# Issuing the scatters of output rows one step later, behind GpSimd's next weight split

## The chip, the cores and the metric

One core of a Trainium2 chip. The metric is device time in microseconds (us), median of the runs; lower is better. The engines are named as the profile names them: PE (TensorE, matmuls), DVE (VectorE), ACT (ScalarE), POOL (GpSimd), SP (SyncE, which issues most of the DMAs).

## What is computed

A causal convolution over 7 positions with softmaxed weights per head, then a mixture of 8 experts with a fixed capacity. Each of the 28,672 tokens goes to one expert, chosen greedily by the gate's logits; every expert takes 3,584 tokens and runs a two-layer network on them. Cut to what matters:

```python
x = conv(x, softmax(weight))               # (28672, 192)
logits = x @ w_gate                        # (28672, 8)
assigned = greedy(logits, cap=28672 // 8)  # best logit first, one expert a token
for e in range(8):
    mask = assigned == e
    h = np.maximum(x[mask] @ w1[e], 0.0)   # w1: 192 x 1024
    out[mask] = h @ w2[e]                  # w2: 1024 x 192
```

## The kernel before

**The three parts.** From 0 to about 175 us the kernel convolves 16 blocks of rows into a DRAM buffer `attn` and computes the gate's logits. Then come the experts' networks, to the end. The routing (thresholds, lists of token numbers) is a background job, cut into pieces which a planner (`Pace`, `Steps`) sets in between the matmuls of the other two parts, until some 670 us. The planner counts what PE, DVE and ACT have to do by a table of costs; it doesn't count POOL.

**The tiles.** `FFN.run` (L1294) goes over 56 tiles of 512 tokens of one expert. The order of the tiles is written out by hand: first one tile of each expert (tiles 0 to 7), since only the tokens that are sure of their expert are listed by then, then the others in runs of an expert. Every engine takes its instructions in the order in which the program issues them.

**One tile, eight steps.** In iteration i, step f (0 to 7) issues: layer 1 of tile i for 128 of the 1,024 hidden units (`l1`: five matmuls into `ph`, a ReLU on ACT that writes `hh`, and on DVE the rest `hl`, for products in two parts of reduced precision); a step of the preparation of tile i + 1 (`prep`: gathered rows are transposed and split into `xa`, `xd`); half a block of layer 2 of tile i - 1 (`l2`: eight matmuls into `y`). Background work goes in between. At the end of each step comes one weight split (`wsplit`), if one is due.

**Gathers and scatters.** Both are indirect DMAs, and POOL issues them (they stand in POOL's queue and take about 1 us of it each). `gather` (L1174, its DMAs at L1179) fetches the 512 rows of tile i + 2 at the head of iteration i, four DMAs into one of two buffers `xg`. `store` (L1240) ends a block of 128 tokens of tile i - 1 in steps 1, 3, 5 and 7: ACT copies one half of `y` to `yt`, DVE adds the other and writes `yo` (three buffers), and POOL scatters `yo` to the output's rows (L1247).

**Weight splits.** The weights are loaded as float32 and split into a high and a low part. A piece (128 x 512 or 128 x 384 elements) goes through one of four buffers `raw`: SP issues its load (L1115 to L1120), ACT writes the high part, POOL or DVE subtracts it and writes the low part (L1160), SP copies both to DRAM for a later use by the same expert, and the load of the piece four further on is issued, into the buffer that is free now. An expert has eight pieces. They are split in the first eight iterations alone, one in each step: in steps 0 to 3 the four pieces of layer 2 (POOL's), in 4 to 7 the pieces of the next expert's layer 1 (POOL's in 4 and 6, DVE's in 5 and 7, `dl`). Later the experts' split weights are read back from DRAM without POOL.

So in the first iterations POOL's queue holds four gathers, four scatters and six splits for each tile, and a scatter stands in it at the end of the step's layer 2, ahead of that step's split. A scatter at the head of the queue waits for its `yo`.

Of the kernel before, what the change touches and what calls it, by code (L numbers as in the profile page):

```python
# [28 lines left out]
class Meter:  # L29


    def __init__(self, pace, name, eng):
        self.pace, self.name, self.eng = pace, name, eng
# [40 lines left out]
class Steps:  # L74
# [6 lines left out]
    def run(self, n=1):  # L81

        for _ in range(n):
            while len(self.gens) > self.keep:
                v = next(self.gens[0], self)
                if v is not self:
                    break
                self.gens.pop(0)
            else:
                return  # L90
            p = self.pace
            self.need = p.dve + p.lat if v == PEW else max(p.dve, p.act) + p.lat if v == PEA else v
# [965 lines left out]
class FFN:  # L1058
# [3 lines left out]
    def __init__(self, tc, nc, attn, w1, w2, out, ident, wr, drm):  # L1062
        self.tc, self.nc = tc, nc

        self.kept1 = [drm.tile([128, 3, F], F32, name="kw%d" % e) for e in range(NE)]
        self.keptd = [drm.tile([64, F], F32, name="kd%d" % e) for e in range(NE)]
        self.kept2 = [drm.tile([128, 8, 2 * D], F32, name="kv%d" % e) for e in range(NE)]
        self.attn, self.w1, self.w2, self.out, self.ident, self.wr = attn, w1, w2, out, ident, wr
        self.bg = lambda: None
        self.busy = lambda: False  # L1070
        self.WT, self.RAW, self.XG, self.XT, self.H, self.Y, self.XS = {}, {}, {}, {}, {}, {}, {}
        self.wpa, self.wpb, self.DL = [None, None], [None, None], [None, None]
        self.scat = []
        self.free = set()
        self.xg = None

# [163 lines left out]
    def store(self, i, b, idx):  # L1240
        nc = self.nc
        y = self.Y.pop((i, b))
        t = self.op.tile([128, D], F32, name="yt", bufs=2)
        o = self.op.tile([128, D], F32, name="yo")
        nc.scalar.activation(t, y[:, D:2 * D], AF.Copy)
        nc.vector.tensor_tensor(o, y[:, 0:D], t, op=OP.add)
        st = nc.gpsimd.indirect_dma_start(  # L1247
            out=self.out, out_offset=bass.IndirectOffsetOnAxis(ap=idx, axis=0), in_=o, in_offset=None,
            bounds_check=NTOK - 1, oob_is_err=False)
        for s in self.scat:  # L1250
            self.tc.declare_no_dep(st.ins, s.ins, reason="rows of other tokens")
        self.scat.append(st)
# [41 lines left out]
    def run(self, idx_of, at, eng, free):  # L1294


        tiles = self.tiles
        n = len(tiles)
        for i in range(n + 1):
            at(i)  # L1300
            if i + 2 < n:
                self.gather(i + 2, idx_of(tiles[i + 2], True))
            for f in range(8):
                if i < n:
                    self.l1(i, tiles[i][0], f)
                self.bg()
                if i + 2 < n and f == 6 and free():
                    self.free.add(i + 2)
                if i + 1 < n:
                    self.prep(i + 1, f)  # L1310
                if i:
                    self.l2(i - 1, tiles[i - 1][0], f // 2, f % 2)
                    if f % 2:
                        self.store(i - 1, f // 2, idx_of(tiles[i - 1])[f // 2])
                        if f == 7:
                            self.H.pop(i - 1)
                self.bg()
                if i < n:
                    self.wsplit(i, eng(f))

# [241 lines left out]
```

## Time and profile before

| | |
|---|---|
| Time, median of 3 runs | 1320.28 us (1318.41 to 1320.54) |
| The profiled execution's own time | 1319.91 us |
| Its span in the profile | 1318.1 us |
| PE busy | 1253.2 us, 95% of the span |
| DVE busy | 1001.2 us, 76% |
| ACT busy | 547.7 us, 42% |
| POOL busy | 544.8 us, 41% |
| Granted PE clock, mean | 0.98 |

A row of the profile's timeline gives the start and the length of an instruction, its engine, its line, its operation and `output<-inputs`, and in brackets how long the engine had been idle ahead of it and what ended that. Nearly all rows of PE, DVE and ACT carry L55, the line of the helper that records them; they are told apart by the names of their tiles. The time of a scatter or gather on POOL is that of its issue; the transfer follows. A matmul's time is modelled, and PE's clock is lowered after it has been idle.

### The profile page before, as it was taken

Reading aid. Unit: us, or ns where it says so; the run is one execution under the profiler, and the core shown is the slowest. Engines: PE = TensorE matmul, PEld = TensorE weight load, DVE = VectorE, ACT = ScalarE, POOL = GpSimd, SP = SyncE. Lnnn points to the kernel's source line nnn. Section 1 sums busy time; section 2 is a strip of 40 time slices with the busy share of each in tenths; the row PEclk is TensorE's granted clock in tenths of the full one; section 3 lists DMA queues with packets and bytes.
Section 4 is the critical chain, followed back from the end, with each engine's and each line's share of the span. In section 5 each row is a group of like instructions: output and inputs, shape, how many; then the busy total and the mean of one; then the engine's idle time right before and its main releaser. Section 6 shows DMA issues by size and latency. Waiting matters only on the chain.

```text
span 1318.1 us, 21815 instructions
## 1 busy us (share of the span) xinstructions
PE 1253.2 (95%) x7879; PEld 1076.2 (82%) x7879; DVE 1001.2 (76%) x2215; ACT 547.7 (42%) x1214; POOL 544.8 (41%) x549
## 2 busy tenths in 40 slices
PE   5789979989899999999999999999999999999997
PEld 3345558878788888888889999999999999999997
DVE  6478558769899988998657777777777777777772
ACT  5444543565444443443333333334333343333432
POOL 3000446476643434534224444444444444444422
PEclk9989998999899999999999999999999999999999
DMA  9999977488742432433222441432323222141100
GB/s 241 302 287 300 295 257 253 156 269 271 228 167 93 149 134 94 149 117 116 73 84 93 139 148 48 149 102 87 108 85 101 94 93 90 49 146 49 40 28 30
DMA packets 92932, 188.30 MB, mean 143 GB/s; under 512 B 12353, under 2 KB 57873, under 8 KB 88593
## 3 DMA queue, kind: packets, MB, share of 16 engines
q1 hardware_dynamic: 63888, 120.75, 29.4%
q0 software_dynamic: 21504, 44.07, 11.0%
q10 hardware_dynamic: 7424, 22.02, 4.4%
q8 instruction: 63, 1.03, 0.3%
q14 instruction: 53, 0.43, 0.1%
HBM read 114.44 MB, written 72.35 MB: 142 GB/s over the span
## 4 chain that ended last, share of the span: by engine, by line
PE 79%; DVE 9%; DMA 4%; issue 3%; SPq 2%; POOL 1%; ACT 1%; POOLq 0%; DVEq 0%; ACTq 0%
PE ph L55 35%; PE y L55 35%; PE bg L55 4%; PE cv L55 3%; DVE X L55 3%; DMA X<-in_x_dram 2%; DVE hl L55 2%; DMA raw<-in_moe_w_dram 1%; PE pl L55 1%; PE px L55 1%; DVE aT L55 1%; SPq L187 1%; DMA attn<-a 1%; SPq L167 1%; SPq L190 1%
## 5 line engine op out<-in xcount | busy, mean ns | idle before, releaser
L55 PE MATMUL y<-w,hh 128*128 128x384 f32 x1792 | 546.6, 360 | 0.0
L55 ACT ACTIVATE hh<-ph 128x512 fp32r<-128x512 f32 x448 | 267.4, 597 | 487.6 <-PE ph L55 389.0
L55 PE MATMUL y<-w,hl 128*128 128x192 f32 x1792 | 452.4, 252 | 0.0
L55 DVE SCALAR_TENSOR_TENSOR hl<-ph,hh 128x512 fp32r<-128x512 f32 x448 | 307.7, 688 | 177.4 <-ACT hh L55 145.7
L55 PE MATMUL ph<-xa,w 128*128 128x512 f32 x1344 | 399.4, 405 | 9.4 <-DVE hl L55 9.4
L55 PEld LDWEIGHTS y<-w,hh 128*128 128x128 f32 x1792 | 341.1, 190 | 25.1 <-issue 7.2
L55 PEld LDWEIGHTS y<-w,hl 128*128 128x128 f32 x1792 | 345.6, 193 | 15.4
L1247 POOL DMA_INDIRECT out_dram<-yo,ib x128 | 128.4, 1003 | 293.4 <-DVE yo L55 278.6
L55 PEld LDWEIGHTS ph<-xa,w 128*128 128x128 f32 x1344 | 221.5, 191 | 30.3 <-DVE hl L55 10.7
L1247 POOL DMA_INDIRECT out_dram<-yo,ia x96 | 106.9, 1113 | 247.3 <-DVE yo L55 213.8
L55 DVE STREAM_TRANSPOSE xs<-xg 32x256 f32<-32x256 f32 (+1 forms) x512 | 188.7, 369 | 8.8
L55 PE MATMUL ph<-xd,w 128*128 128x512 f32 x448 | 179.5, 401 | 1.6 <-DVE xd L55 1.1
L55 PE MATMUL ph<-xd,dl 128*128 128x512 f32 x448 | 176.9, 395 | 2.5 <-DVE dl L55 2.2
L1179 POOL DMA_INDIRECT xg<-attn,jb x128 | 130.0, 1016 | 40.1 <-issue 39.8
L55 PE MATMUL cv<-X,TH 118*128 118x384 f32 x256 | 103.1, 528 | 22.2 <-DVE TH L55 12.8
L1179 POOL DMA_INDIRECT xg<-attn,ja x96 | 107.8, 1123 | 28.9 <-issue 25.2
L55 ACT ACTIVATE yt<-y 128x192 f32<-128x192 f32 x224 | 73.2, 327 | 109.0 <-PE y L55 97.8
L55 DVE TENSOR_TENSOR yo<-y,yt 128x192 f32<-128x192 f32 x224 | 79.5, 355 | 47.4 <-ACT yt L55 43.0
L55 PEld LDWEIGHTS ph<-xd,dl 128*128 128x128 f32 x448 | 85.1, 190 | 24.1 <-DVE dl L55 3.8
L55 PEld LDWEIGHTS ph<-xd,w 128*128 128x128 f32 x448 | 84.9, 190 | 22.9 <-DVE xd L55 1.8
L55 PEld LDWEIGHTS cv<-X,TH 118*128 118x128 f32 x256 | 46.0, 200 | 55.0 <-issue 22.6
L55 ACT ACTIVATE a<-cv 128x384 f32<-128x384 f32 x128 | 61.5, 490 | 58.0 <-PE cv L55 51.7
(235 smaller groups left out, 974.0 us busy)
## 6 DMA issues: line engine op xcount, KB each, us to landing
w<-kw SPq DMA_DIRECT2D x16, 1536.0 KB
w<-kv SPq DMA_DIRECT2D x16, 1536.0 KB
X<-in_x_dram SPq DMA_DIRECT2D x16, 1344.0 KB
attn<-a ACTq DMA_DIRECT2D x16, 1344.0 KB
kw<-w SPq DMA_DIRECT2D x48, 256.0 KB
kv<-w SPq DMA_DIRECT2D x32, 384.0 KB
raw<-in_moe_w_dram SPq DMA_DIRECT2D x32, 192.0 KB
raw<-in_moe_w_dram SPq DMA_DIRECT2D x16, 256.0 KB
```

Source lines behind the costliest of these rows:

```text
L55: return f(*a, **k)
L167: nc.sync.dma_start(wgr[32 * pb:32 * pb + 32], wg.rearrange("(c f) e -> f c e", f=32))
L187: nc.sync.dma_start(t[0:6, 1:16], bass.AP(tensor=x.tensor, offset=o + (W - 6) * D, ap=[[D, 6], [W * D, 15], [1, D]]))
L190: nc.sync.dma_start(t[0:6], bass.AP(tensor=x.tensor, offset=o - 6 * D, ap=[[D, 6], [W * D, 16], [1, D]]))
L1179: self.nc.gpsimd.indirect_dma_start(out=t[:, b], out_offset=None, in_=self.attn[0:rows], in_offset=bass.IndirectOffsetOnAxis(ap=idx[b], ax ...
L1247: st = nc.gpsimd.indirect_dma_start(out=self.out, out_offset=bass.IndirectOffsetOnAxis(ap=idx, axis=0), in_=o, in_offset=None, bounds_chec ...
```

## The change

`store` no longer issues the scatter. It puts `yo` and its row numbers into a list, and a new function `scatter` takes them from there and issues the DMA. `run` calls it at the end of the even steps, after that step's weight split. So the scatter of step 1 is issued in step 2, that of step 3 in step 4, that of step 5 in step 6, and that of step 7 in step 0 of the next iteration, behind that iteration's four gathers. In the iteration behind the last tile, the one of step 7 is issued in step 7 itself.

```diff
@@ __init__
-        self.scat = []
+        self.scat, self.late = [], []
@@ store
         nc.vector.tensor_tensor(o, y[:, 0:D], t, op=OP.add)
-        st = nc.gpsimd.indirect_dma_start(
+        self.late.append((o, idx))
+
+    def scatter(self):
+
+        if not self.late:
+            return
+        o, idx = self.late.pop()
+        st = self.nc.gpsimd.indirect_dma_start(
             out=self.out, out_offset=bass.IndirectOffsetOnAxis(ap=idx, axis=0), in_=o, in_offset=None,
             bounds_check=NTOK - 1, oob_is_err=False)
@@ run, at the end of a step
                 if i < n:
                     self.wsplit(i, eng(f))
+                if not f % 2 or i == n and f == 7:
+                    self.scatter()
```

The order of the instructions on PE, DVE, ACT and SP is the same as before; POOL's alone changes. There, in the second iteration that has both scatters and splits, stood before (L1160 is a split, `w2` a piece of layer 2 and `w1` one of layer 1; L1247 is a scatter of the `yo` with that number; `x4` stands for a tile's four gathers):

```order
L1160 TENSOR_TENSOR w2_2392<-raw_2234,w2_2392 128x2x192
L1247 DMA out_0_dram<-yo_2456,ia0_105 28672x192
L1160 TENSOR_TENSOR w2_2392<-raw_2266,w2_2392 128x2x192
L1160 TENSOR_TENSOR w2_2392<-raw_2292,w2_2392 128x2x192
L1247 DMA out_0_dram<-yo_2581,ia0_105 28672x192
L1160 TENSOR_TENSOR w2_2392<-raw_2325,w2_2392 128x2x192
L1160 TENSOR_TENSOR w1_2672<-raw_2396,w1_2672 128x512
L1247 DMA out_0_dram<-yo_2698,ia0_105 28672x192
L1160 TENSOR_TENSOR w1_2672<-raw_2531,w1_2672 128x512
L1247 DMA out_0_dram<-yo_2794,ia0_105 28672x192
L1179 DMA xg_2806<-attn_62,ja0_109 128x192 x4
L1160 TENSOR_TENSOR w2_2839<-raw_2677,w2_2839 128x2x192
```

and there stands now, at the same place of POOL's queue (the scatters have L1254; the numbers of `yo` are the same in both, those of the other tiles are a few lower):

```order
L1160 TENSOR_TENSOR w2_2389<-raw_2231,w2_2389 128x2x192
L1254 DMA out_0_dram<-yo_2315,ia0_105 28672x192
L1160 TENSOR_TENSOR w2_2389<-raw_2263,w2_2389 128x2x192
L1160 TENSOR_TENSOR w2_2389<-raw_2289,w2_2389 128x2x192
L1254 DMA out_0_dram<-yo_2456,ia0_105 28672x192
L1160 TENSOR_TENSOR w2_2389<-raw_2322,w2_2389 128x2x192
L1160 TENSOR_TENSOR w1_2669<-raw_2393,w1_2669 128x512
L1254 DMA out_0_dram<-yo_2581,ia0_105 28672x192
L1160 TENSOR_TENSOR w1_2669<-raw_2528,w1_2669 128x512
L1254 DMA out_0_dram<-yo_2698,ia0_105 28672x192
L1179 DMA xg_2803<-attn_62,ja0_109 128x192 x4
L1160 TENSOR_TENSOR w2_2836<-raw_2674,w2_2836 128x2x192
```

The pattern looks alike, but each place holds the scatter of one block earlier: `yo_2456` now comes behind two more splits, `yo_2581` and `yo_2698` behind the next splits of theirs, and `yo_2794` behind the four gathers and the split that follow here. In a later tile, which has no splits, POOL's queue held:

```order
L1247 DMA out_0_dram<-yo_6408,ia_106 28672x192
L1179 DMA xg_6414<-attn_62,ja_110 128x192 x4
L1247 DMA out_0_dram<-yo_6505,ia_106 28672x192
L1247 DMA out_0_dram<-yo_6554,ia_106 28672x192
L1247 DMA out_0_dram<-yo_6607,ia_106 28672x192
L1247 DMA out_0_dram<-yo_6664,ia_106 28672x192
L1179 DMA xg_6675<-attn_62,ja_110 128x192 x4
```

and holds now:

```order
L1179 DMA xg_6411<-attn_62,ja_110 128x192 x4
L1254 DMA out_0_dram<-yo_6408,ia_106 28672x192
L1254 DMA out_0_dram<-yo_6505,ia_106 28672x192
L1254 DMA out_0_dram<-yo_6554,ia_106 28672x192
L1254 DMA out_0_dram<-yo_6607,ia_106 28672x192
L1179 DMA xg_6672<-attn_62,ja_110 128x192 x4
L1254 DMA out_0_dram<-yo_6664,ia_106 28672x192
```

There a tile's last scatter, `yo_6408` and `yo_6664`, and the four gathers have changed places, and nothing else.

## The prediction, made before the run

> **What bounds the kernel now.** I read the table of windows first, to find where TensorE (PE) is not full; then the waits of the stretch that is left; then, in the timeline, what ended each of its longer waits. The columns of the windows are the stretch, its length, busy us of PE, PE's weight load, VectorE (DVE), ScalarE (ACT) and GpSimd (POOL), the granted clock, the DMA share and GB/s.
>
> ```profile
> 200.00:230.00 30.00, 27.49 (x186) 23.92 (x187) 24.32 (x47) 10.86 (x23) 18.32 (x16) 0.83 0.75 241
> 230.00:300.00 70.00, 62.87 (x400) 54.84 (x398) 51.06 (x97) 41.90 (x107) 39.87 (x35) 0.94 0.67 219
> 300.00:400.00 100.00, 92.21 (x518) 81.90 (x518) 93.55 (x214) 44.91 (x104) 61.44 (x55) 0.96 0.65 211
> 700.00:800.00 100.00, 100.00 (x571) 90.84 (x570) 77.24 (x169) 37.87 (x76) 45.02 (x46) 1.00 0.38 125
> ```
>
> From 700 on PE is full at full clock, and POOL has nothing left but gathers and scatters, so there is nothing for the change to win there. The weight splits lie before 400, and there PE is short of work and of clock. The clock's loss between 200 and 400 is worth 30 x 0.17 + 70 x 0.06 + 100 x 0.04 = 13.3 us (an estimate, since the clock of a window is a mean). The waits between 170 and 420 us (who waited for whom: us, times, longest) and PE's first long one:
>
> ```profile
> POOL out_dram L1247 <- DVE yo L55: 62.4, 22, 6.6
> ACT w L55 <- DMA raw<-in_moe_w_dram: 31.8, 23, 4.3
> DVE hl L55 <- ACT hh L55: 24.9, 14, 6.2
> PE ph L55 <- DVE hl L55: 9.4, 3, 4.2
> PE bg L55 <- DVE r_cc L55: 7.5, 3, 5.6
> PE bg L55 <- DVE oa L55: 2.2, 2, 1.7
> DVE yo L55 <- ACT yt L55: 6.9, 3, 4.9
> ...
> 175.61 1.65 PE L55 MATMUL ph<-xa,w 128*128 128x512 f32 x3 [4.24 <-DVE hl L55]
> ```
>
> PE's three groups add up to 19.1 us; the 4.24 at 175.61 is before the first scatter and stays, which leaves 14.9 us of idle PE that the change could reach. With the 13.3 of clock the ceiling of any gain is 28.2 us.
>
> **What is moved.** POOL's work in the same stretch, by group (count | busy us, mean ns | idle before):
>
> ```profile
> L1179 POOL DMA_INDIRECT xg<-attn,ja x44 | 51.0, 1158 | 13.1 <-issue 12.4 <-DMA kd<-dl 0.6
> L1247 POOL DMA_INDIRECT out_dram<-yo,ia x37 | 43.2, 1167 | 71.9 <-DVE yo L55 62.4 <-DMA raw<-in_moe_w_dram 2.5 <-DVE T L55 1.9
> L1160 POOL TENSOR_TENSOR w<-raw,w 128x384 fp32r<-128x384 f32 x32 | 33.2, 1054 | 1.0 <-ACT w L55 0.4
> L1160 POOL TENSOR_TENSOR w<-raw,w 128x512 fp32r<-128x512 f32 x14 | 18.1, 1295 | 11.8 <-ACT w L55 11.7
> ```
>
> A tile has four gathers, four scatters and six splits on POOL: 4 x 1.16 + 4 x 1.17 + 4 x 1.05 + 2 x 1.30 = 16.1 us (with 0.3 of issue ahead of each gather, 17.3). PE needs 104 matmuls for a tile's two layers, which at the 571 in 100 us of the full stretch is 18.2 us. So POOL just fits, as long as it does not wait; but its scatters wait 62.4 us for yo, and each time the queue behind them stands.
>
> The change takes no instruction away and adds none. After it, the scatter of step 1 stands behind the splits of steps 1 and 2, that of step 3 behind those of 3 and 4, that of step 5 behind that of 6, and that of step 7 behind the next tile's four gathers and its first split. By the time a scatter is reached its yo should be there. Most of the 62.4 us then becomes time in which splits and gathers run.
>
> **Term 1: the late weight load.** Here is one waiting scatter, followed through to PE:
>
> ```profile
> 255.31 2.93 POOL L1247 DMA_INDIRECT out_dram<-yo,ia  x1 [6.03 <-DVE yo L55]
> 256.83 0.52 ACT L55 ACTIVATE w<-raw 128x384 fp32r<-128x384 f32 x1
> 258.54 1.98 POOL L1179 DMA_INDIRECT xg<-attn,ja  x1 [0.30 <-issue]
> ...
> 264.47 1.04 POOL L1160 TENSOR_TENSOR w<-raw,w 128x384 fp32r<-128x384 f32 x1
> 265.91 0.42 SPq L1115 DMA_DIRECT2D raw<-in_moe_w_dram  x1
> ...
> 269.05 0.63 ACT L55 ACTIVATE w<-raw 128x512 fp32r<-128x512 f32 x1 [3.38 <-DMA raw<-in_moe_w_dram]
> 271.98 0.58 ACT L55 ACTIVATE hh<-ph 128x512 fp32r<-128x512 f32 x1
> 272.59 0.69 DVE L55 SCALAR_TENSOR_TENSOR hl<-ph,hh 128x512 fp32r<-128x512 f32 x1 [6.20 <-ACT hh L55]
> 273.34 0.97 PE L55 MATMUL ph<-xa,w 128*128 128x512 f32 x3 [2.60 <-DVE hl L55]
> ...
> 275.82 2.08 PE y L55 x8
> 279.54 1.12 PE y L55 x8
> ```
>
> The scatter of a tile's last block holds POOL until 258.24; four gathers follow; and the split whose ScalarE half was done at 257.35 runs at 264.47. Its raw buffer is free only then, so the load into it is issued at 265.91, ScalarE waits 3.38 us for a load, the ReLU behind that (hh) and VectorE's hl come late, and PE stops for 2.60. In the new order the gathers stand behind the scatter of step 5 and may start two steps sooner, and the split waits for neither. I take the whole 2.60 off. The eight matmuls at 275.82 took 2.08 where the same eight took 1.12 at 279.54; that is the clock after a stop, and it is counted below.
>
> **Term 2: VectorE held while POOL runs.** Some VectorE operations take far longer when splits run on POOL beside them. The first pair below is one operation twice, the second pair another one twice; then two more such places, and PE behind each:
>
> ```profile
> 326.37 1.09 DVE L55 TENSOR_TENSOR X<-r_w,m_f 128x896 bf16<-128x896 f32 x1
> 332.52 3.65 DVE L55 TENSOR_TENSOR X<-r_w,m_f 128x896 bf16<-128x896 f32 x1
> 333.24 1.97 POOL L1160 TENSOR_TENSOR w<-raw,w 128x384 fp32r<-128x384 f32 x2
> 328.24 1.01 DVE L55 TENSOR_TENSOR X<-X 128x448 bf16<-128x448 bf16 x3
> 336.36 3.75 DVE L55 TENSOR_TENSOR X<-X 128x448 bf16<-128x448 bf16 x3
> 337.75 2.23 POOL L1160 TENSOR_TENSOR w<-raw,w 128x384 fp32r<-128x384 f32 x2
> 340.45 0.21 PE L55 MATMUL bg<-r_cc,ones 128*128 128x56 bf16 x1 [5.58 <-DVE r_cc L55]
> ...
> 291.71 3.22 DVE L55 TENSOR_TENSOR X<-X,c_mu 128x512 bf16<-128x512 f32 x1
> 292.09 2.28 POOL L1160 TENSOR_TENSOR w<-raw,w 128x384 fp32r<-128x384 f32 x2
> 297.39 0.97 PE L55 MATMUL ph<-xa,w 128*128 128x512 f32 x3 [2.58 <-DVE hl L55]
> ...
> 213.04 2.81 DVE L55 TENSOR_TENSOR oa<-irep,q 128x1024 bf16<-128x1024 bf16 x2
> 215.31 1.27 PE L55 MATMUL bg<-X,oa 128*128 128x16 bf16 x16 [1.69 <-DVE oa L55]
> ```
>
> The operations at 332.52 and 336.36 took 2.56 and 2.74 us longer than their twins, 5.3 together, which is nearly all of PE's 5.58. Both times POOL ran two splits back to back, released together by a scatter. Without waiting scatters the splits follow ScalarE one by one, and an operation that meets one is held for 1.05, not for two in a row; but it may meet one more often. I take half of the 5.58, of the 2.58 and of the 1.69: 2.8 + 1.3 + 0.8 = 4.9 us. The ends of this term are all of it, 9.9, and below nothing, as much again lost to new meetings (third rival).
>
> The Trainium skill (SBUF — State Buffer, "Who interferes with whom") says that VectorE in certain modes and GpSimd share one pair of ports as an exclusive lock, and that issue order decides who blocks. The rows above agree. By that rule alone the same splits hold the lock for as long as before, term 2 would be 0, and the time 4.9 us above the forecast.
>
> **The clock.** Of the 14.9 us of idle PE I take 2.6 + 4.9 = 7.5. Much of the slow clock does not directly follow a stop (it is 0.83 in 200:230, where the stop is 1.69), so I take a quarter of the 13.3 us with it: 3.3. Its ends are nothing and all.
>
> **What costs nothing.** A scatter now leaves later, and its yo buffer is one of three. The buffer is written again three blocks, or six steps, later, some 13.6 us at 18.2 us for eight steps. The worst place is step 7's scatter: four gathers and a split, 4 x 1.46 + 1.05 = 6.9 us, are ahead of it if they have not yet run; the scatter's 1.17 follows, and 5.5 us are left for it to land. No wait of VectorE's yo for a scatter stands among the waits above (the only one is for ScalarE's yt), so I take 0; without that slack it would be a stop of VectorE once a tile. The four gathers pass one scatter and gain time; their buffer was last read in step 4 of the tile before. SyncE's and ScalarE's queues keep their order: the copies of the split weights and the next loads can only start sooner. After 400 us only the last scatter of a tile changes place, under a full PE: 0. The last tile has no gathers and no splits, so the end is the old one: 0.
>
> **Sum.** 2.6 + 4.9 + 3.3 = 10.8 us. The profiled execution took 1319.91 (span 1318.1), so 1309.1; the median of the runs is 0.37 above that execution, so 1309.5.
>
> **Rivals.**
>
> *VectorE takes it back (no change).* In 300:400 VectorE is busy 93.55 of 100 us. If it sets the pace from 285 to 390, PE reaches each of its results sooner and waits there; term 1 is lost behind the next backlog and term 2 stays. For it: PE's longest wait, 5.6, is for VectorE. Against: VectorE waited 24.9 us for hh, and it was idle for 18.9 of the 70 us in 230:300. Time 1318 to 1322.
>
> *The splits come apart and hold VectorE more often (slower).* Waiting scatters bunched the splits; now about 40 single ones are spread over seven tiles. If ten more VectorE operations meet one at 1.05 us each and PE waits for all of it, that is 10.5; against term 1 with its clock, some 3.5, the sum is +7, 1327. It decides if the meetings rise by more than about four. For it: in 300:400 VectorE has 6 us to spare. Against: what a split costs when met would fall from two in a row to one.
>
> *Nearly all of it falls (much faster).* If all the idle time goes and most of the clock's loss, 20 to 26 us: 1294 to 1300. For it: the stops feed each other. Against: the 5.58 hangs on VectorE, not on POOL's order.
>
> **How the numbers follow.** Forecast (1302 to 1317): 0.62. No change: 0.18. Slower: 0.10. Much faster: 0.10. A measurement of this kernel can tell about 0.2%, 2.6 us, from no change. Faster by more than that: 0.62 + 0.10 = 0.72; same 0.18; slower 0.10. The range must hold the forecast, no change and the near edge of much faster: 1299 to 1321; it leaves out the slower case and the rest of the fastest, under 2 in 10.
>
> **What would show it.** Right: the scatters' wait for yo between 170 and 420 falls from 62.4 to under 20, ScalarE's for raw from 31.8 to under 15, PE's stop of 2.60 behind a raw load is gone, and PE's idle time in 200 to 400 falls from 17.4 (the windows) by some 7. Wrong: POOL waits less but PE's idle time is the same, now under VectorE's operations; or a yo waits for a scatter's landing; or the time moves after 400.

## The result, and the profile after

| | before | after |
|---|---|---|
| Time, median (runs) | 1319.96 us (7) | 1308.70 us (7) |
| Lowest and highest | 1316.72 to 1320.93 | 1305.86 to 1314.52 |
| The profiled execution's own time | 1319.91 us | 1309.36 us |
| Its span | 1318.1 us | 1307.3 us |
| PE, DVE, POOL busy in it | 1253.2, 1001.2, 544.8 us | 1247.7, 1005.3, 556.1 us |

The ratio is 0.993, with a 95% interval of 0.9914 to 0.9946: faster by 9.2 us, by 7.1 to 11.4. The forecast was 1309.5.

The windows after, with the columns of the prediction's first fence:

```profile
200.00:230.00 30.00, 29.02 (x219) 25.54 (x215) 25.34 (x48) 12.85 (x26) 19.63 (x14) 0.89 0.85 278
230.00:300.00 70.00, 64.48 (x398) 57.44 (x397) 55.86 (x102) 45.41 (x116) 45.67 (x39) 0.95 0.70 229
300.00:400.00 100.00, 92.12 (x526) 81.93 (x525) 96.50 (x214) 47.61 (x113) 56.48 (x52) 0.97 0.58 193
700.00:800.00 100.00, 100.00 (x571) 90.81 (x570) 76.16 (x163) 38.23 (x76) 47.92 (x46) 1.00 0.34 114
```

From 700 nothing has changed, as expected. Between 200 and 400 PE is idle 14.4 us where it was 17.4, and its clock is a little higher in each of the three windows. VectorE is still nearly full in the last of them, busy for 96.5 of 100 us.

The waits between 170 and 420 us:

```profile
POOL out_dram L1254 <- DVE yo L55: 39.9, 14, 5.5
POOL w L1160 <- ACT w L55: 37.8, 17, 8.2
...
DVE hl L55 <- ACT hh L55: 19.6, 11, 6.6
ACT w L55 <- DMA raw<-in_moe_w_dram: 17.2, 15, 4.5
...
PE bg L55 <- DVE r_cc L55: 5.7, 2, 5.3
...
PE ph L55 <- DVE hl L55: 3.9, 1, 3.9
...
PE px L55 <- issue: 3.5, 1, 3.5
...
PE px L55 <- DVE xa L55: 2.1, 1, 2.1
```

Of before, one more row of that view:

```profile
POOL w L1160 <- ACT w L55: 12.1, 6, 4.2
```

GpSimd now waits more for the right thing, ScalarE's half of a split (37.8 us, from 12.1), and less for yo (39.9, from 62.4). ScalarE's wait for raw has fallen from 31.8 to 17.2. PE's stops behind hl are gone but for the one of 3.9 ahead of the first scatter. Its stop for r_cc has not moved: 5.3 beside 5.6. Two new ones have come, of 3.5 and 2.1 us, for px, the bank into which gathered rows are transposed.

Windows at fixed times hold different work in the two kernels. PE has the same instructions in the same order in both, so a stretch can be cut between the same two matmuls: from the routing's `ones,F`, just ahead of the first scatter, to its first 120-wide `r_cc,ones`, just behind the last split. In before, and then in after:

```profile
194.84:380.56 185.72, 168.74 (x1030) 148.46 (x1030) 155.13 (x320) 93.71 (x225) 115.34 (x100) 0.93 0.74 241
```

```profile
192.74:371.09 178.35, 164.13 (x1029) 145.50 (x1028) 155.83 (x320) 95.41 (x227) 115.98 (x100) 0.94 0.76 253
```

The stretch is 7.4 us shorter: 2.8 less of idle PE (16.98 to 14.22), and 4.6 less for the same matmuls, which I put down to the clock (0.94, from 0.93). Within it the scatters' wait for yo is 13.0 us, from 46.0. VectorE's busy time in it is the same, 155.1 and 155.8. Of the 10.8 us between the two spans the remaining 3.4 lie outside: 2.1 ahead of the first scatter and 1.3 behind the last split. In the profiles of all the runs below that keep PE's order the first matmul of the stretch comes between 193.1 and 197.8 us, whichever kernel it is, so I don't count those 2.1.

### The profile page after: what moved, and what is told of

The parts are those of the page before. It is cut to its first block, busy times and chain, and to the rows that moved or that the text cites. A ratio compares the mean times of both kernels' runs of the same rounds, so it can differ in the third digit from the quotient of the medians.

```text
span 1307.3 us, 21815 instructions
## 1 busy us (share of the span) xinstructions
PE 1247.7 (95%) x7879; PEld 1072.5 (82%) x7879; DVE 1005.3 (77%) x2215; ACT 551.0 (42%) x1214; POOL 556.1 (43%) x549
## 4 chain that ended last, share of the span: by engine, by line
PE 80%; DVE 9%; DMA 5%; issue 2%; SPq 1%; ACT 1%; POOL 1%; POOLq 0%; DVEq 0%; ACTq 0%
PE ph L55 36%; PE y L55 35%; PE bg L55 3%; DVE X L55 3%; PE cv L55 3%; DMA X<-in_x_dram 3%; DVE hl L55 2%; PE px L55 1%; PE pl L55 1%; DVE aT L55 1%; DMA wgr<-in_moe_w_gate_dram 1%; DMA attn<-a 1%; DMA raw<-in_moe_w_dram 1%; DVE oa L55 1%; SPq L187 0%
## 5 line engine op out<-in xcount | busy, mean ns | idle before, releaser
L55 PEld LDWEIGHTS y<-w,hl 128*128 128x128 f32 x1792 | 343.4, 192 | 15.2
L1254 POOL DMA_INDIRECT out_dram<-yo,ib x128 | 128.4, 1003 | 287.7 <-DVE yo L55 277.5
L1254 POOL DMA_INDIRECT out_dram<-yo,ia x96 | 105.4, 1098 | 205.0 <-DVE yo L55 169.0
L1179 POOL DMA_INDIRECT xg<-attn,jb x128 | 138.2, 1080 | 40.9 <-issue 40.9
L1179 POOL DMA_INDIRECT xg<-attn,ja x96 | 111.8, 1164 | 29.0 <-issue 26.7
L1160 POOL TENSOR_TENSOR w<-raw,w 128x384 fp32r<-128x384 f32 (+1 forms) x48 | 54.1, 1137 | 72.7 <-ACT w L55 37.8
```

Source lines behind the costliest of these rows:

```text
L55: return f(*a, **k)
L1160: eng.tensor_tensor(lo, r[0:n], hi[0:n].bitcast(F32), op=OP.subtract)
L1179: self.nc.gpsimd.indirect_dma_start(out=t[:, b], out_offset=None, in_=self.attn[0:rows], in_offset=bass.IndirectOffsetOnAxis(ap=idx[b], ax ...
L1254: st = self.nc.gpsimd.indirect_dma_start(out=self.out, out_offset=bass.IndirectOffsetOnAxis(ap=idx, axis=0), in_=o, in_offset=None, bounds ...
```

## The experiments

They ran in three batches, on chips on which the kernel before had medians of 1313.91 (first four), 1314.21 (next four) and 1321.56 us (last four). So each is set against the kernel before of its own batch, by the ratio of the runs; the profile of each is one execution. Most of these took within 2.6 us of their kernel's median. Two did not, and both are the fastest of their kernel's twelve: step 7's took 1307.60 us, 5.8 under its median, and the one with a VectorE split given to GpSimd 1309.86, 6.9 under. The right half of their rows stands for a faster execution than the left half. "Idle" and "busy" are PE's within the stretch defined above; the last two columns are the waits between 170 and 420 us.

| what leaves later | median, before's | ratio (95%) | stretch us | idle | busy | POOL for yo | ACT for raw |
|---|---|---|---|---|---|---|---|
| nothing (before, first pair) | 1319.96 | 1 | 185.7 | 17.0 | 168.7 | 62.4 | 31.8 |
| all four (after, first pair) | 1308.70, 1319.96 | 0.9930 (0.9914 to 0.9946) | 178.4 | 14.2 | 164.1 | 39.9 | 17.2 |
| all, early tiles only | 1306.62, 1313.91 | 0.9949 (0.9927 to 0.9970) | 176.6 | 13.7 | 162.9 | 39.0 | 18.0 |
| step 7's | 1313.42, 1313.91 | 0.9989 (0.9969 to 1.0009) | 180.3 | 17.2 | 163.1 | 67.4 | 26.7 |
| steps 1, 3 and 5 | 1308.21, 1313.91 | 0.9958 (0.9942 to 0.9974) | 176.6 | 12.1 | 164.5 | 42.9 | 27.9 |
| all, behind own split | 1314.69, 1313.91 | 1.0007 (0.9990 to 1.0025) | 184.6 | 14.6 | 170.1 | 59.0 | 29.9 |
| nothing; fifth raw buffer | 1311.16, 1314.21 | 0.9974 (0.9960 to 0.9987) | 182.4 | 17.1 | 165.4 | 58.7 | 13.7 |
| all, by two steps | 1306.81, 1314.21 | 0.9954 (0.9936 to 0.9973) | 175.0 | 13.3 | 161.7 | 35.3 | 15.2 |
| all; a VectorE split to GpSimd | 1316.71, 1314.21 | 1.0015 (0.9996 to 1.0035) | 179.8 | 16.4 | 163.4 | 39.6 | 19.8 |
| all; fifth raw buffer | 1305.28, 1314.21 | 0.9927 (0.9906 to 0.9948) | 175.1 | 13.7 | 161.5 | 38.6 | 7.8 |
| step 5's | 1321.83, 1321.56 | 0.9996 (0.9973 to 1.0019) | 183.2 | 15.8 | 167.3 | 45.5 | 27.2 |
| steps 1 and 3 | 1321.34, 1321.56 | 0.9994 (0.9976 to 1.0011) | 181.7 | 13.9 | 167.8 | 50.2 | 27.1 |
| all, by two; fifth raw buffer | 1308.93, 1321.56 | 0.9910 (0.9881 to 0.9939) | 174.5 | 12.4 | 162.0 | 37.4 | 7.6 |
| all four (after), third batch | 1312.85, 1321.56 | 0.9935 (0.9911 to 0.9958) | 174.5 | 13.4 | 161.1 | 36.7 | 20.3 |

All of these but the run with the VectorE split given to GpSimd keep the order of PE, VectorE and ScalarE; those with a fifth buffer also move SyncE's loads.

**Only the early tiles.** The late scatters end with the splits:

```diff
-                if not f % 2 or i == n and f == 7:
+                if not f % 2 or i > 7:
                     self.scatter()
```

> The scatters leave late only in the iterations that have splits (up to the seventh); behind them the order is the one of before. Queue theory (the gain comes from splits and gathers that no longer stand behind a waiting scatter while PE is short of work): nearly all of the gain is there, 1309 to 1312 us. Rival, the gathers' place behind 400 us (there the profile pair differs by 2.1 us more): without it 2 to 4 us are lost, 1312 to 1314.

0.9949, or 6.7 us faster, and its interval holds the whole effect. What lies behind the stretch (the span less the stretch's end) takes 931.3 us in this profile and 931.2, 931.1 and 931.3 in the other three of the batch. Only the first of those three, step 7's, has the scatter's new place behind the gathers in all tiles. So nothing is gained or lost behind the last split, and the rival falls.

**The halves: step 7 alone, and steps 1, 3 and 5.** The scatter is issued in `run`, right behind `store`, where it isn't to be late:

```diff
                         self.store(i - 1, f // 2, idx_of(tiles[i - 1])[f // 2])
+                        if f < 7:
+                            self.scatter()
...
-                if not f % 2 or i == n and f == 7:
+                if f == 0 or i == n and f == 7:
                     self.scatter()
```

> Only the scatter of step 7 is issued later, behind the next tile's gathers and first split; those of steps 1, 3 and 5 stay in their own step. Queue theory: the stop of 2.60 us behind a late raw load hung on a step 7 scatter and the four gathers behind it, so this part alone gives 3 to 6 of the 11 us, 1314 to 1317, and ScalarE's wait for raw (31.8 us between 170 and 420) falls to about 22. Meeting theory (what counts is which VectorE operations meet a split): the parts are not tied to a step; anything from 1309 to 1320, and it need not add up with the other half.

0.9989: 1.4 us faster, between 4.1 faster and 1.2 slower, so none to be told; 3 to 6 were expected, and ScalarE's wait for raw fell to 26.7, not to 22. The complement (`if f == 7` behind `store`, `if not f % 2` at the step's end):

> The complement: the scatters of steps 1, 3 and 5 leave one step later, that of step 7 in its own step ahead of the gathers. Queue theory: 4 to 7 of the 11 us, 1312.5 to 1316, and with the run of step 7 alone the two gains add up to 9 to 13. Meeting theory: the sum of the two gains is off by more than 4 us from the whole.

0.9958: 5.5 us faster (3.4 to 7.6). The halves add up to 6.9 beside 8.6 and 9.2 of the whole, well within their intervals; the expectation had the halves nearer to equal, and their sum at 9 to 13. The two stops that the prediction followed can be told apart here. With step 7's scatter left in its place, the one behind the late raw load is there as it was. From the timeline of that run:

```profile
251.56 2.93 POOL L1254 DMA_INDIRECT out_dram<-yo,ia  x1 [4.14 <-DVE yo L55]
...
265.31 0.63 ACT L55 ACTIVATE w<-raw 128x512 fp32r<-128x512 f32 x1 [3.39 <-DMA raw<-in_moe_w_dram]
...
269.59 0.73 PE L55 MATMUL ph<-xa,w 128*128 128x512 f32 x2 [2.60 <-DVE hl L55]
```

The scatter waits, ScalarE waits 3.39 us for raw, and PE stops for 2.60, the same as before. That stop is 2.5 to 2.7 us in every run that leaves step 7's scatter ahead of the gathers with four raw buffers (before, own split, this one, step 5, steps 1 and 3), and none where it is late. So its cause is shown, and yet this run, which keeps it, is the faster half.

**Behind its own split.** `scatter()` is called at the end of every step.

> Each scatter stays in its step but goes behind that step's split; so the splits of steps 1 and 3 are freed, those of steps 2, 4 and 6 and the gathers still stand behind a waiting scatter. Queue theory: a third of the gain, 1315 to 1318, the scatters' wait for yo between 170 and 420 stays above 45 us. Meeting theory: not tied to the wait; 1309 or 1320 are as likely.

1.0007: no gain, where a third of the whole was expected. The wait for yo stays at 59.0 us. A single split let past is not enough; the rest of the queue still stands.

**Raw buffers instead of late scatters.** A fifth buffer, and one more load issued at the start; the scatters as before:

```diff
-        wr = pool(cw, "wr", 4)
+        wr = pool(cw, "wr", 5)
...
-                for _ in range(4):
+                for _ in range(5):
                     ff.wload()
```

> The kernel before with a fifth raw buffer and one more load ahead; the scatters stay in their places. Raw-load theory (a late split hurts through the raw buffer that it frees late, so that ScalarE waits for the next load and hh behind it): ScalarE's wait for raw between 170 and 420 falls from 31.8 to under 15 us and most of the gain comes without moving a scatter, 4 to 8 us faster than before. Rival (a late split hurts by when it runs, beside which VectorE operation, and not by its buffer): ScalarE waits less and the time is within 2 us of before.

0.9974: 3.4 us faster (1.7 to 5.3), just under what the raw-load theory wanted. ScalarE's wait for raw falls to 13.7, less than in the changed kernel, and the stop behind it to half. The row of PE at that place:

```profile
271.72 0.73 PE L55 MATMUL ph<-xa,w 128*128 128x512 f32 x2 [1.24 <-POOL w L1160]
```

So the late buffer is a part of the cost, some 3 us, and not most of it: steps 1, 3 and 5 gain 5.5 while ScalarE waits 27.9 for raw.

**Two steps later.** The list is a queue, and a scatter leaves at the end of the next odd step:

```diff
-        o, idx = self.late.pop()
+        o, idx = self.late.pop(0)
...
-                if not f % 2 or i == n and f == 7:
-                    self.scatter()
+                if f % 2:
+                    if len(self.late) > 1:
+                        self.scatter()
+                    if i == n and f == 7:
+                        self.scatter()
```

> Each scatter leaves two steps later instead of one, with the same three yo buffers. Queue theory: nothing of weight is left behind a waiting scatter after one step, so the time is within 3 us of the run with the late scatters in the early tiles alone, 5 to 9 us faster than before. Rival, the three yo buffers: a scatter that leaves at the end of step 3 has four steps less its landing until its buffer is written again; if that is too short, VectorE waits at yo and the time is up to 5 us over that run.

0.9954, 6.0 us faster. No wait of VectorE for a scatter's landing appears, so three yo buffers are enough even for two steps.

**A VectorE split given to GpSimd.** `VP = (3,)` for `VP = (1, 3)` in the changed kernel.

> The changed kernel with one of the two VectorE splits of a tile (64 x 512, 0.67 us) given to GpSimd (1.28 us). VectorE theory (what is left of the stops between 200 and 390 is VectorE's backlog): 7 x 0.67 = 4.7 us of VectorE's work leave the stretch, 2 to 4 us faster than the changed kernel. Meeting theory: a seventh split a tile holds VectorE more than it relieves it; 0 to 4 us slower.

1.0015: the gain is gone, which is more than the 4 us that the meeting theory would have lost. VectorE was rid of six operations of 0.67 us and yet busy for 159.9 us in the stretch, not 155.8. But the planner counts VectorE's work and not GpSimd's, so it also set the background pieces elsewhere (PE's and VectorE's orders differ), and it took 2.7 us more behind the stretch than others of its batch. It speaks for the meeting theory and does not settle it.

**The changed kernel with a fifth raw buffer.** The edit is that of the fifth buffer above.

> The changed kernel with a fifth raw buffer and one more load ahead. Raw-load theory: the 17.2 us that ScalarE still waits for raw fall under 8, and 1 to 3 us more are gained than by the changed kernel. Rival: ScalarE waits less and nothing is gained, since the stops that are left hang on VectorE.

0.9927. ScalarE's wait for raw is down to 7.8, and the gain of 9.6 us (6.8 to 12.4) can't be told from the changed kernel's 9.2 or 8.6.

**Step 5 alone.** This takes out the stop of 1.69 us for oa alone:

```diff
+                        if f != 5:
+                            self.scatter()
...
-                if not f % 2 or i == n and f == 7:
+                if f == 6:
                     self.scatter()
```

> Only the scatter of step 5 leaves one step later, behind the split of step 6; the other three stay in their steps. Meeting theory for one place: the wait of 1.69 us for oa near 215 us is in every run in which step 5's scatter holds back the split of step 6 (that split then runs beside the first oa) and in none where it does not. So here it is gone and 2 to 5 us are gained. Rival (that stop is made up behind the next one): the wait is gone and the time is within 1.5 us of before.

GpSimd, VectorE and PE at that place:

```profile
211.83 1.55 POOL L1160 TENSOR_TENSOR w<-raw,w 128x512 fp32r<-128x512 f32 x1 [2.44 <-ACT w L55]
...
215.06 1.27 DVE L55 TENSOR_TENSOR oa<-irep,q 128x1024 bf16<-128x1024 bf16 x2
...
215.79 1.27 PE L55 MATMUL bg<-X,oa 128*128 128x16 bf16 x16 [0.16 <-DVE oa L55]
```

and in the run that moves steps 1 and 3 instead (`if f > 4` behind `store`, `if f in (2, 4)` at the step's end):

> The scatters of steps 1 and 3 leave one step later, those of steps 5 and 7 stay. If the parts of the gain add up, this gives what steps 1, 3 and 5 together gave (5.5 us) less the gain of step 5 alone: 1 to 3 us; the wait of 1.69 us for oa near 215 is there as before. Rival (which split meets what decides, and parts do not add): off that sum by more than 3 us.

```profile
215.37 2.79 DVE L55 TENSOR_TENSOR oa<-irep,q 128x1024 bf16<-128x1024 bf16 x2
215.72 1.28 POOL L1160 TENSOR_TENSOR w<-raw,w 128x512 fp32r<-128x512 f32 x1
...
217.61 1.28 PE L55 MATMUL bg<-X,oa 128*128 128x16 bf16 x16 [1.67 <-DVE oa L55]
```

With step 5's scatter late, the split of step 6 is done at 213.38 and two oa take 1.27 us. With it in place the split runs at 215.72, beside the first oa, the two take 2.79, and PE stops for 1.67. That stop, of 1.67 to 1.69, is in all five kernels that leave step 5's scatter in place (before, step 7, own split, the fifth buffer alone, and this one) and in none of the others with the planner's order kept. So this cause is shown as well. But neither run is faster: 0.9996 and 0.9994, with intervals of 3.0 and 2.3 us to either side. What came is the rival of the first of them: the stop is gone, and no gain is to be told. Their sum, 1.3 us, is under the 5.5 of steps 1, 3 and 5 together; the difference of 4.2 is about as large as its uncertainty.

**Both, and the changed kernel once more.** Two steps late with a fifth raw buffer, and the changed kernel on the same chip:

> Scatters two steps later and a fifth raw buffer with one more load ahead. Queue theory: the two take away different waits (GpSimd's for yo, ScalarE's for raw), so this is the fastest, 1 to 4 us under the changed kernel. Rival: what is left hangs on VectorE's backlog, and it is within 1.5 us of the changed kernel.

> The changed kernel itself, on the chip of the runs beside it, so that their parts can be set against the whole: 7 to 11 us faster than before.

0.9910 (0.9881 to 0.9939) and 0.9935 (0.9911 to 0.9958). The medians are 1308.93 and 1312.85: the combination has the lowest ratio of all and is 3.9 us under the changed kernel by the medians, though the intervals overlap.

## Why the prediction was right, point by point

**The total** (10.8 us; 9.2 measured, and 8.6 on another chip) was right, and so was the stretch in which it lies: the run with late scatters in the early tiles alone and the equal times behind the stretch show it. The single terms were not.

**Term 1, the late raw load (2.6).** The mechanism was right: the stop of 2.60 hangs on step 7's scatter, and a fifth buffer halves it. What failed is "I take the whole 2.60 off". In its place there is now a stop for px, close behind. From the timeline of the changed kernel in the third batch:

```profile
278.04 2.99 DVE L55 SCALAR_TENSOR_TENSOR X<-LT,c_T 128x256 f32<-128x256 f32 x2
...
278.80 1.94 POOL L1160 TENSOR_TENSOR w<-raw,w 128x384 fp32r<-128x384 f32 x2
...
281.56 0.67 DVE L55 TENSOR_TENSOR xa<-px,xa 128x512 fp32r<-128x512 f32 x1
...
282.38 1.03 PE L55 MATMUL px<-ident,xg 128*64 128x128 f32 x4 [3.56 <-DVE xa L55]
```

Two splits back to back on GpSimd hold VectorE's X operations for 2.99 us, xa behind them is late, the transposes' bank is not read yet, and PE stops for 3.56 (3.46 in the first profile of the changed kernel). The second new stop for px, in that profile, looks the same. One operation there takes 0.68 us when free, and 2.38 beside two splits:

```profile
344.68 0.68 DVE L55 TENSOR_TENSOR X<-X,X 128x512 f32<-128x512 f32 x1
...
345.71 2.00 POOL L1160 TENSOR_TENSOR w<-raw,w 128x384 fp32r<-128x384 f32 x2
...
345.88 2.38 DVE L55 TENSOR_TENSOR X<-X,X 128x512 f32<-128x512 f32 x1
...
350.47 0.60 PE L55 MATMUL px<-ident,xg 128*64 128x128 f32 x4 [2.07 <-DVE xa L55]
```

Step 7's half alone is worth 1.4, not to be told from nothing. This is the first rival's mechanism, VectorE taking it back, at two places.

**Term 2, VectorE held (4.9).** Two of its three stops went, against half of each in the sum: the 1.69 for oa to 0.15, and the 2.58 behind hl. The third and largest, 5.58 for r_cc, stayed at 5.29, and it is 2.6 to 6.0 us in each run at about the same place except for the one that moved the planner's pieces. The stops that the prediction named, term 1's with them, fell by 7.0 us, near its 7.5. The step that failed is that new stops stand at nothing in the sum (they are in the term's lower end alone): the two for px are 5.5 us. Behind it is "without waiting scatters the splits follow ScalarE one by one", which came true for half of them. Splits stood back to back on GpSimd in eleven pairs in the stretch before, and in six pairs and one row of three after. Nor was it a waiting scatter that kept these together. The one ahead of the pair at 318.80 below waited 0.17 us; what made the queue late were the four gathers ahead of it, behind which a split whose ScalarE half was done at 312.94 ran at 316.52. The scatter ahead of the prediction's first pair by r_cc, at 333.24, had waited 0.17 us too, so that "released together by a scatter" was misread there. So holding has moved to other operations and not fallen. Four groups of VectorE's in the stretch (count | busy, mean ns | idle ahead of it), in before and then in after:

```profile
L55 DVE TENSOR_TENSOR X<-X,c_mu 128x512 bf16<-128x512 f32 x8 | 10.6, 1356 | 0.0
...
L55 DVE SCALAR_TENSOR_TENSOR X<-LT,c_T 128x256 f32<-128x256 f32 x16 | 6.8, 477 | 0.1
...
L55 DVE TENSOR_TENSOR X<-r_w,m_f 128x896 bf16<-128x896 f32 x2 | 4.7, 2372 | 0.1
...
L55 DVE TENSOR_TENSOR X<-X,X 128x512 f32<-128x512 f32 x4 | 2.6, 680 | 0.0
```

```profile
L55 DVE SCALAR_TENSOR_TENSOR X<-LT,c_T 128x256 f32<-128x256 f32 x16 | 11.6, 775 | 0.1
...
L55 DVE TENSOR_TENSOR X<-X,X 128x512 f32<-128x512 f32 x4 | 6.4, 1610 | 0.0
...
L55 DVE TENSOR_TENSOR X<-X,c_mu 128x512 bf16<-128x512 f32 x8 | 5.2, 683 | 0.0
...
L55 DVE TENSOR_TENSOR X<-r_w,m_f 128x896 bf16<-128x896 f32 x2 | 2.2, 1091 | 0.1
```

The first and third of before are at their free speed now, 683 and 1091 ns; the second and fourth of before have become slow by about as much (8.6 us more for the two, 7.9 less for the others). VectorE's whole busy time in the stretch is 155.1 and 155.8. The prediction named the Trainium skill's rule on this (SBUF — State Buffer, "Who interferes with whom": an exclusive lock, decided by issue order) and said that by it the term would be 0. For VectorE's busy time that was so in this pair, and the new stops for px took most of term 2 back. It is not a rule that holds whatever the order: the same stretch kept VectorE busy for 149.3 us with steps 1, 3 and 5 late and for 158.6 with step 7's late (one profile each). What the rows say of the order stands in the last section. And for PE it matters which operation is held: one that PE needs at once, as oa, or one with slack.

At r_cc itself the hold has only moved ahead. From the timeline of after:

```profile
315.88 1.71 DVE L55 TENSOR_TENSOR r_tl<-T,Ts 128x8 f32<-128x8 f32 x1
...
317.72 1.05 POOL L1254 DMA_INDIRECT out_dram<-yo,ia  x1 [0.17 <-DMA raw<-in_moe_w_dram]
...
318.10 2.74 DVE L55 TENSOR_TENSOR X<-j,r_dd 128x56 f32<-128x56 f32 x1
...
318.80 1.95 POOL L1160 TENSOR_TENSOR w<-raw,w 128x384 fp32r<-128x384 f32 x2
...
321.33 1.09 DVE L55 TENSOR_TENSOR X<-r_w,m_f 128x896 bf16<-128x896 f32 x1
...
324.54 0.21 PE L55 MATMUL bg<-r_cc,ones 128*128 128x56 bf16 x1 [5.29 <-DVE r_cc L55]
```

The operation that took 3.65 before takes 1.09 here. But two small ones ahead of it took 1.71 and 2.74 us, the second beside two splits, where they take 0.14 and 0.22 when free. That is 4.1 us of holding, beside 5.3 before, and PE's stop behind the chain is 5.29 beside 5.58.

**Idle PE and the clock.** The sum had 7.5 us of idle and 3.3 of clock. Against the one profile of before, the two profiles of the changed kernel have 2.8 and 3.6 us less idle time in the stretch, and 4.6 and 7.6 less of PE's busy time for the same matmuls. So the idle term was sized more than twice too large, by the new stops. Whether the clock's was too small is less sure. The traces show that PE's clock is not a little lower for long, but half for 3.41 us at a time, in one piece or two. Windows cut along such pieces, the clock third from the end: two in before, one in after, and two of the changed kernel in the third batch:

```profile
274.36:277.77 3.41, 3.10 (x11) 2.65 (x11) 1.91 (x4) 3.03 (x9) 2.50 (x2) 0.50 1.00 339
339.21:346.04 6.83, 5.59 (x19) 5.10 (x19) 5.91 (x14) 1.96 (x4) 2.39 (x3) 0.50 0.83 279
```

```profile
322.51:329.34 6.83, 4.80 (x17) 4.05 (x17) 6.55 (x16) 1.86 (x4) 2.01 (x2) 0.50 0.55 190
```

```profile
326.27:329.68 3.41, 3.41 (x13) 2.74 (x12) 3.24 (x9) 1.73 (x4) 1.41 (x2) 0.50 1.00 341
329.68:371.19 41.51, 39.45 (x233) 35.17 (x232) 40.77 (x88) 20.76 (x51) 24.46 (x22) 1.00 0.70 234
```

The first stands behind the stop of 2.60, the others at the stop for r_cc: it brought two pieces in before and in after, and one in the third batch, with full clock behind it. The stretch has eight such pieces in before, six in after and three in the third batch, at 1.7 us of lost clock each. So what a stop costs in clock differs between executions of one kernel, and single profiles do not size this term. Over all executions the mean granted clock was 0.9785 for before and 0.9823 for the changed kernel in the third batch, and 0.9801 for before and 0.9816 for the early tiles alone in the first. On some 1310 us that is about 5 and about 2 us (estimates from these means), and 3.3 lies between. "A quarter of the 13.3" was no more than a choice, and that the total came so near with an idle term that was too large is luck. What makes a stop cost one piece, two or none stays open.

The five kernels with all four scatters late by one or two steps and the planner's order kept show 161.1 to 164.1 us of busy PE (the changed one twice); step 5 alone, steps 1 and 3, and own splits show 167.3 to 170.1. Step 7 alone has 163.1, but in an execution 5.8 us under its median, so that row doesn't speak for the kernel.

**What costs nothing** held: no yo waits for a scatter, the gathers come in time, nothing changes behind the last split. Three of the four signs were put too high. The scatters' wait for yo fell to 39.9 and not under 20, since 26.9 of it lie between the last split and 420 us, where it is harmless (16.4 before); ScalarE's for raw fell to 17.2 and not under 15; and PE's idle time between 200 and 400 fell by 3.0 and not by 7. The fourth, the stop of 2.60, is gone as it said.

**The rivals.** "VectorE takes it back" is true of px and of r_cc, but not of the time. "The splits come apart and hold VectorE more often" is half true: the VectorE operations of the stretch that took over 0.3 us longer than the shortest of their kind in any run rose from 12 to 19, all of them beside a split. That is more than the four at which the rival was to decide, but they are held for 21.8 us together, beside 21.5, and the time fell (17 and 19.4 us in the third batch). What carries the gain is best told by which moves showed it: steps 1, 3 and 5 together (5.5 us), not step 5 (0.5), not 1 and 3 (0.8), not a place behind the own split (none). GpSimd's queue has 17.3 us of work for a tile that takes PE 18.2 or more, so one scatter that still waits makes it late for what follows. That reading fits all runs; it was argued from them, and the single parts' intervals are too wide to prove that they don't add up.

## What to carry to other kernels

In a queue that is taken in order, an instruction that waits costs what stands behind it, not what it does itself: look at who needs the entries behind it, and put the one whose input is late behind those whose inputs are there. A stop that can be traced to its cause need not be worth its length: two here, of 2.60 and 1.69 us, were each removed by a single edit that moved the time by less than could be told (their lengths lie within the intervals), and of the moves of scatters only those of three or four, by a step or more, gave a gain that can be told. Look also for the stops that come in place of the one that goes. When two engines hold each other up, count their held time over the whole stretch, and ask for each held operation who waits for it.

## What the runs showed of the hardware

An issue of an indirect DMA on GpSimd, usually 1.0 us, can itself take several times as long. From the timeline of after, a gather beside five oa in a row:

```profile
214.68 4.01 POOL L1179 DMA_INDIRECT xg<-attn,ja  x1 [0.30 <-issue]
```

```profile
214.73 3.08 DVE L55 TENSOR_TENSOR oa<-irep,q 128x1024 bf16<-128x1024 bf16 x5
```

It took 4.01 us, and ended 0.9 behind the last of them. Of the thirteen profiles with the planner's order, twelve have such a gather at this place: it takes 2.80 to 4.01 us and ends 0.9 behind the five oa. In that of step 7 alone it doesn't: the two gathers beside them take 1.16 and 1.50.

A held VectorE operation can begin ahead of the split that it is held beside. The one at 318.10 above, 0.22 us long when free, begins 0.70 ahead of the pair, while GpSimd issues the scatter at 317.72; and of the prediction's held operations, the one at 332.52 begins 0.72 ahead of its pair. So these rows bear out that the two engines shut each other out, but not that the one which starts first goes first. The scatter's issue alone does not explain it: in the same profile two oa at 210.86 took 1.28 us, their free speed, beside the scatter issued from 210.03 to 211.22.

And the same instructions behind the stretch, with PE busy for 98 to 99% of the time and at a clock of 0.99 to 1.00, took 931.1 to 931.3 us in the four profiles of one batch and 938.1 to 940.0 in those of another, on another chip. So a difference of 1% between batches has to be taken out before parts of 0.3% can be told.
